# Queries and keys brought feature-first by the host; their low parts taken from SBUF by GpSimd

## The chip, the cores and the metric

One core of a Trainium2 chip. The metric is the device time of one execution in microseconds. The engines are TensorE (PE in the rows; PEld is its weight load), VectorE (DVE), ScalarE (ACT), GpSimd (POOL) and SyncE (SP), which issues all loads and stores.

## What is computed

Attention over 2 batches, 8 heads, 768 positions and 64 features per head, with a window of 96 earlier keys and 8 global ones, and then two products with a nonlinear middle for 1536 tokens of 512 features:

```python
scores = scale * q @ k^T + bias            # bias: -slope[h] * distance
scores = where(local or global, scores, -1e9)
a = exp(scores - max); a = a / (sum(a) + 1e-9)
x = a @ v                                  # heads side by side: [1536, 512]
h = x @ w_in;  x = (h * cos(h)) @ w_out    # 512 -> 2048 -> 512
out = ((x @ w_a) * (x @ w_b)) @ w_out2     # 512 -> 1536 -> 512
```

The weights are 64-bit floats in DRAM, and the kernel turns them into 32-bit ones in blocks. All products are made in parts: a value is split into a high part that TensorE takes and a low part, the rest, and the products of high with high, high with low and low with high are summed.

## The kernel before

The attention runs over 12 tiles of 128 positions, 6 for a batch. Each tile goes through steps that have short names, and a table gives each step a time, counted in tiles from the tile's own. The steps of all tiles are written in the order of these times, and TensorE, GpSimd, VectorE and ScalarE keep the written order. SyncE is not held to it: its loads are placed by the scheduler, where a buffer comes free. An engine's instruction that waits holds up all behind it.

For tile i, `LQ`, `LK`, `LV` load q, k and v as [128 positions, 8 heads, 64] (tiles nq and nk with two buffers, nv with one). `SQ` (`scale_q`) multiplies q by a factor for each head on GpSimd. `TQ` and `TK` (`turned`) transpose four pairs of heads of q and of k into PSUM on TensorE. `QH`, `KH` (`q_hi`, `k_hi`) copy that to the high parts on ScalarE. `QL`, `KL` (`q_lo`, `k_lo`) subtract the high part from the transposed value, which gives the low part. GpSimd does not read PSUM here, so QL on GpSimd needs a second copy:

```python
if QP[0] <= i < QP[1]:
    nc.scalar.activation(out=qc_of[i], in_=tq, func=AF.Copy)
```

QP is (3, 13): tiles 3 to 11 have this copy (qc) on ScalarE and QL on GpSimd; QL of tiles 0 to 2 and KL of all tiles read PSUM on VectorE. The keys of two neighbouring tiles lie in the two halves of kx. `FK` keeps the first keys of a batch in kg, and `PK`, once the scores of a tile are done, puts them in place of that tile's own first keys; both are on GpSimd. `S0` and `S1` are the scores of the two halves of the heads on TensorE; S0 of tile i + 1 needs QL and KL of i + 1 and PK of i. `B`, `E`, `T`, `H`, `L`, `P` are, for four pairs of heads each, the bias (VectorE), the exponential (ScalarE), the transpose of the weights (TensorE, tile tp), its two parts (ScalarE, VectorE) and the product with V (TensorE). `V` (`split_v`) makes three parts of V on GpSimd (tile vx; vg holds a batch's first ones, and `VG` is a DMA of them). `RL`, `FIN`, `TX`, `XH`, `XL` end the tile: VectorE, VectorE, TensorE, ScalarE, VectorE. Tile 0 is done in halves, with times of its own (`START`), and `first_bias` with the counts n_global and n_local (`read_counts`) stands between the halves on VectorE.

Between these steps the first weight blocks are loaded (raws, raw) and converted: two copies on ScalarE, four operations on VectorE (cv), and a subtraction on GpSimd (wl). Behind the attention the two products (`moe`) run, with the rest of the blocks converted as they are needed. A second, general attention exists for larger windows and is not entered with these inputs.

Of the kernel before, what the change touches and what calls it, by code (L numbers as in the profile page):

```python
# [29 lines left out]
QP = (3, 13)  # L30
# [2 lines left out]
TABLE = {'S0': -0.894, 'T3': 0.134, 'TX': 1.203, 'TQ': -1.895, 'P0': 0.161, 'TK': -1.643, 'S1': -0.525, 'P1': 0.341, 'T0': -0.22, 'T1': -0.233, 'P2': 0.506, 'P3': 0.588, 'T2': -0.085, 'RL': 0.846, 'FIN': 0.963, 'L2': 0.298, 'B0': -0.757, 'B1': -0.676, 'L3': 0.443, 'XL': 1.457, 'B2': -0.371, 'B3': -0.219, 'KL': -1.201, 'L0': 0.036, 'L1': -0.108, 'H2': 0.02, 'H3': 0.339, 'XH': 1.381, 'E0': -0.666, 'E1': -0.347, 'QH': -1.59, 'KH': -1.325, 'E2': -0.243, 'H0': -0.146, 'H1': -0.218, 'E3': -0.066, 'SQ': -2.793, 'V': -0.869, 'PK': -0.368, 'QL': -1.371, 'FK': -1.121, 'VG': 1.106, 'LQ': -4.408, 'LK': -2.688, 'LV': -1.259}
# [4 lines left out]
START_OPS = "SQ TQ QH QL TK KH KL".split()  # L38
START = ((-2.99, -2.98, -2.97, -2.96, -2.95, -2.94, -2.93), (-2.92, -2.91, -2.9, -2.86, -2.89, -2.88, -2.85))
# [8 lines left out]
def tile_kernel(ctx, tc, q, k, v, n_global, n_local, w_in, w_out, w_a, w_b, w_out2, out):  # L48
    nc = tc.nc
    B, H, S, D = q.shape  # L50
# [119 lines left out]
    qc_of = {}  # L170

    def q_hi(i, tq, hps=ALL):
        if i not in q_of:
            q_of[i] = at.tile([P, 2, HP, P], F32R, tag="qT", name=f"qT{i}", bufs=2)
        nc.scalar.activation(out=q_of[i][:, 0, hps], in_=tq, func=AF.Copy)
        if QP[0] <= i < QP[1]:
            qc_of[i] = at.tile([P, HP, P], F32, tag="qc", name=f"qc{i}", bufs=1)
            nc.scalar.activation(out=qc_of[i], in_=tq, func=AF.Copy)

    def q_lo(i, tq, hps=ALL):  # L180
        qT = q_of[i]
        if i in qc_of:
            pool_sub(qT[:, 1], qc_of.pop(i), f(qT[:, 0]))
        else:
            nc.vector.tensor_tensor(out=qT[:, 1, hps], in0=tq, in1=f(qT[:, 0, hps]), op=ALU.subtract)

    def k_hi(i, tk, hps=ALL):
        nc.scalar.activation(out=kx[:, i % 2, 0, hps], in_=tk, func=AF.Copy)

# [623 lines left out]
```

## Time and profile before

| what | value |
|---|---|
| median of 3 runs | 732.5 us (732.21 to 733.02) |
| profiled execution: span from first to last instruction | 731.0 us |
| TensorE busy, share of the span | 676.8 us, 93% |
| VectorE busy | 510.7 us, 70% |
| ScalarE busy | 303.3 us, 41% |
| GpSimd busy | 289.8 us, 40% |

The profile gives no time of its own for the profiled execution beside the span. The shares are averages over stages that differ: the attention ends near 120 us, then comes a stretch to about 260 us in which weights are converted beside the first products, and after it the products alone. What an engine is worth has to be read in its stage. TensorE's products are pipelined and their ends modelled, so that its durations overlap; the distance from one start to the next says what a group costs.

### The profile page before, as it was taken

Reading aid. Unit: us, or ns where it says so; the run is one execution under the profiler, and the core shown is the slowest. Engines: PE = TensorE matmul, PEld = TensorE weight load, DVE = VectorE, ACT = ScalarE, POOL = GpSimd, SP = SyncE. Lnnn points to the kernel's source line nnn. Section 1 sums busy time; section 2 is a strip of 40 time slices with the busy share of each in tenths; the row PEclk is TensorE's granted clock in tenths of the full one; section 3 lists DMA queues with packets and bytes.
Section 4 is the critical chain, followed back from the end, with each engine's and each line's share of the span. In section 5 each row is a group of like instructions: output and inputs, shape, how many; then the busy total and the mean of one; then the engine's idle time right before and its main releaser. Section 6 shows DMA issues by size and latency. Waiting matters only on the chain.

```text
span 731.0 us, 10359 instructions
## 1 busy us (share of the span) xinstructions
PE 676.8 (93%) x3936; PEld 556.5 (76%) x3936; DVE 510.7 (70%) x901; ACT 303.3 (41%) x559; POOL 289.8 (40%) x263
## 2 busy tenths in 40 slices
PE   4899998799885999999989698999999999999996
PEld 3778887588763788788878486888888888888885
DVE  6999898999999979859979715885727322222223
ACT  4798886554445444444454413334314111111110
POOL 5789851664444434425252404435315211111110
PEclk9999999989987799999999799999999999999998
DMA  9944320223333202201303101333301000000004
GB/s 210 249 108 107 81 48 1 86 71 103 98 103 115 87 30 87 87 1 58 105 11 109 64 0 31 106 114 95 117 1 57 1 1 0 1 1 0 1 29 150
DMA packets 65084, 49.80 MB, mean 68 GB/s; under 512 B 39168, under 2 KB 59648, under 8 KB 65024
## 3 DMA queue, kind: packets, MB, share of 16 engines
q1 hardware_dynamic: 65024, 49.04, 23.4%
q8 instruction: 33, 0.54, 0.3%
q14 instruction: 27, 0.22, 0.1%
HBM read 45.09 MB, written 3.15 MB: 66 GB/s over the span
## 4 chain that ended last, share of the span: by engine, by line
PE 50%; DVE 35%; ACT 6%; issue 4%; POOL 2%; DMA 2%; SPq 0%; POOLq 0%; ACTq 0%; DVEq 0%
DVE cv L361 6%; DVE u L436 5%; PE o L502 4%; PE o L503 4%; PE o L501 4%; DVE cv L362 4%; PE b L413 4%; PE b L412 4%; PE b L411 4%; PE a L412 4%; PE a L411 4%; PE a L413 4%; DVE u L435 4%; DVE cv L358 3%; DVE cv L360 3%
## 5 line engine op out<-in xcount | busy, mean ns | idle before, releaser
L138 POOL TENSOR_TENSOR wl<-cv,wh 128x512 fp32r<-128x512 f32 x68 | 97.1, 1431 | 167.1 <-ACT wh L368 163.9
L138 POOL TENSOR_TENSOR glu<-as,ghu 128x512 fp32r<-128x512 f32 x36 | 47.5, 1320 | 158.5 <-ACT ghu L455 158.5
L491 DVE TENSOR_TENSOR as<-b,as 128x512 f32<-128x512 f32 x36 | 24.8, 689 | 117.6 <-PE b L413 116.4
L138 POOL TENSOR_TENSOR gl<-u,gh 128x512 fp32r<-128x512 f32 x48 | 69.8, 1464 | 74.4 <-ACT gh L455 62.3
L411 PE MATMUL h<-xTh,wh 128*128 128x512 f32 x192 | 79.1, 412 | 7.6 <-ACT hs L434 5.8
L473 PE MATMUL y<-gh,wh 128*128 128x512 f32 x192 | 75.4, 393 | 9.2 <-ACT gh L455 9.2
L474 PE MATMUL y<-gl,wh 128*128 128x512 f32 x192 | 76.0, 396 | 6.4 <-POOL gl L138 6.4
L412 PE MATMUL h<-xTl,wh 128*128 128x512 f32 x192 | 79.0, 411 | 0.0
L413 PE MATMUL h<-xTh,wl 128*128 128x512 f32 x192 | 78.6, 409 | 0.0
L475 PE MATMUL y<-gh,wl 128*128 128x512 f32 x192 | 75.2, 392 | 0.0
L368 ACT ACTIVATE wh<-cv 128x512 fp32r<-128x512 f32 x68 | 42.7, 628 | 69.1 <-DVE cv L362 58.2
L440 ACT ACTIVATE u<-u,quarter 128x512 f32<-128x512 f32 x48 | 34.7, 723 | 72.1 <-DVE u L436 72.1
L507 DVE TENSOR_TENSOR oacc<-o,oacc 128x512 f32<-128x512 f32 x60 | 41.2, 690 | 31.6 <-PE o L503 31.6
L411 PE MATMUL a<-yh,wh 128*128 128x512 f32 x144 | 57.2, 398 | 6.3 <-ACT as L488 4.2
L411 PE MATMUL b<-yh,wh 128*128 128x512 f32 x144 | 57.6, 400 | 3.0 <-ACT hs L434 3.0
L488 ACT ACTIVATE as<-a 128x512 f32<-128x512 f32 x36 | 21.4, 593 | 88.6 <-PE a L413 88.6
L361 DVE SCALAR_TENSOR_TENSOR cv<-raw,cv 128x512 int32<-128x512 int32 x62 | 57.4, 926 | 0.9
L412 PE MATMUL a<-yl,wh 128*128 128x512 f32 x144 | 57.1, 396 | 0.6 <-DVE yl L482 0.6
L413 PE MATMUL b<-yh,wl 128*128 128x512 f32 x144 | 57.4, 398 | 0.0
L412 PE MATMUL b<-yl,wh 128*128 128x512 f32 x144 | 57.2, 398 | 0.0
L413 PE MATMUL a<-yh,wl 128*128 128x512 f32 x144 | 57.0, 396 | 0.0
L351 ACT ACTIVATE cv<-raw 128x512 f32<-128x512 f32 x62 | 41.4, 668 | 37.2 <-POOL wl L138 18.0
(106 smaller groups left out, 1540.7 us busy)
## 6 DMA issues: line engine op xcount, KB each, us to landing
raw<-in_moe_w_out_dram SPq DMA_DIRECT2D x26, 512.0 KB, 3.3
raw<-in_moe_w_in_dram SPq DMA_DIRECT2D x12, 512.0 KB, 3.7
raw<-in_moe_w_a_dram SPq DMA_DIRECT2D x12, 512.0 KB, 3.6
raw<-in_moe_w_b_dram SPq DMA_DIRECT2D x12, 512.0 KB, 3.6
nv<-in_v_dram SPq DMA_DIRECT2D x12, 256.0 KB, 4.3
out_dram<-oacc SPq DMA_DIRECT2D x12, 256.0 KB, 2.9
nq<-in_q_dram SPq DMA_DIRECT2D x11, 256.0 KB, 3.6
nk<-in_k_dram SPq DMA_DIRECT2D x11, 256.0 KB, 4.4
```

Of the source, the lines that this page charges most:

```text
L138: nc.gpsimd.tensor_tensor(out=dst, in0=a, in1=b, op=ALU.subtract)
L351: nc.scalar.activation(out=f(c), in_=f(top), func=AF.Abs)
L361: lambda: nc.vector.scalar_tensor_tensor(out=c, in0=top, scalar=-0x40000000, in1=c, op0=ALU.bitwise_and, op1=ALU.bitwise_or),
L368: nc.scalar.activation(out=hi, in_=f(cvs[x]), func=AF.Copy)
L411: nc.tensor.matmul(dst, wh[:, kk, :], xh[:, kk, :], start=(kk == 0), stop=False)
L412: nc.tensor.matmul(dst, wh[:, kk, :], xl[:, kk, :], start=False, stop=False)
L413: nc.tensor.matmul(dst, wl[:, kk, :], xh[:, kk, :], start=False, stop=(kk == KD - 1))
L436: nc.vector.scalar_tensor_tensor(out=u, in0=u, scalar=MAGIC, in1=hs, op0=ALU.subtract, op1=ALU.subtract)
L473: nc.tensor.matmul(yps, wh[:, m, :], gh, start=(x == 0), stop=False)
L474: nc.tensor.matmul(yps, wh[:, m, :], gl, start=False, stop=False)
L475: nc.tensor.matmul(yps, wl[:, m, :], gh, start=False, stop=(x == len(items) - 1))
L507: nc.vector.tensor_tensor(out=acc[:, u, :], in0=ops, in1=acc[:, u, :], op=ALU.add)
```

## The change

The host hands q and k over as [batch, tile, 2 x 64 features of a pair of heads, 4 pairs, 128 positions]. A tile's load is then one run of 2 KB for each of 128 partitions (1 KB for the halves of tile 0) in place of eight runs of 256 bytes, and lies in SBUF as the products need it. TQ and TK are gone, and so are their PSUM tiles and the copies qc. SQ multiplies by a factor that now differs between the upper and lower 64 partitions. QH and KH read nq and nk from SBUF. QL and KL do as well: on VectorE for tile 0, on GpSimd for all others. The buffers of nq and nk are therefore free for the next load only after QL and KL, where before they were free after TQ and TK. All other times of the table are as before. The general attention takes the new layout too.

```diff
-START_OPS = "SQ TQ QH QL TK KH KL".split()
-START = ((-2.99, -2.98, -2.97, -2.96, -2.95, -2.94, -2.93), (-2.92, -2.91, -2.9, -2.86, -2.89, -2.88, -2.85))
+START_OPS = "SQ QH QL KH KL".split()
+START = ((-2.99, -2.97, -2.96, -2.94, -2.93), (-2.92, -2.9, -2.86, -2.88, -2.85))
...
-    def load(nm, i, heads=slice(0, H)):
+    def load(nm, i, hps=slice(0, HP)):
         if i < NT // P:
             b, t = divmod(i, NQ)
             if nm not in nat.setdefault(i, {}):
-                nat[i][nm] = at.tile([P, H, D], F32, tag="n" + nm, name=f"n{nm}{i}", bufs=2 if nm != "v" else 1)
-            nc.sync.dma_start(out=nat[i][nm][:, heads], in_=srcs[nm][b, heads, t * P:(t + 1) * P, :].rearrange("h p d -> p h d"))
+                shape = [P, H, D] if nm == "v" else [P, HP, P]
+                nat[i][nm] = at.tile(shape, F32, tag="n" + nm, name=f"n{nm}{i}", bufs=2 if nm != "v" else 1)
+            if nm == "v":
+                nc.sync.dma_start(out=nat[i][nm], in_=v[b, :, t * P:(t + 1) * P, :].rearrange("h p d -> p h d"))
+            else:
+                nc.sync.dma_start(out=nat[i][nm][:, hps], in_=srcs[nm][b, t, :, hps, :])
...
-    qf = const.tile([P, H], F32, tag="qf", name="qf")
+    qf = const.tile([P, HP], F32, tag="qf", name="qf")
-        nc.gpsimd.memset(qf[:, h:h + 1], qscale / slope[h])
+        nc.gpsimd.memset(qf[(h % 2) * D:(h % 2 + 1) * D, h // 2:h // 2 + 1], qscale / slope[h])
...
     def scale_q(i, hps=ALL):
-        heads = slice(2 * hps.start, 2 * hps.stop)
-        x = nat[i]["q"][:, heads]
-        by = qf[:, heads].rearrange("p (h o) -> p h o", o=1).to_broadcast([P, heads.stop - heads.start, D])
+        x = nat[i]["q"][:, hps]
+        by = qf[:, hps].rearrange("p (h o) -> p h o", o=1).to_broadcast([P, hps.stop - hps.start, P])
         nc.gpsimd.tensor_tensor(out=x, in0=x, in1=by, op=ALU.mult)
 
-    def turned(nm, i, hps=ALL):
-        t = ps.tile([P, hps.stop - hps.start, P], F32, tag="tr", name=f"t{nm}{i}_{hps.start}", bufs=TR)
-        for x, hp in enumerate(range(hps.start, hps.stop)):
-            transpose(t[:, x, :], head(nat[i], nm, hp))
-        return t
-
-    qc_of = {}
-
-    def q_hi(i, tq, hps=ALL):
+    def q_hi(i, hps=ALL):
         if i not in q_of:
             q_of[i] = at.tile([P, 2, HP, P], F32R, tag="qT", name=f"qT{i}", bufs=2)
-        nc.scalar.activation(out=q_of[i][:, 0, hps], in_=tq, func=AF.Copy)
-        if QP[0] <= i < QP[1]:
-            qc_of[i] = at.tile([P, HP, P], F32, tag="qc", name=f"qc{i}", bufs=1)
-            nc.scalar.activation(out=qc_of[i], in_=tq, func=AF.Copy)
-
-    def q_lo(i, tq, hps=ALL):
-        qT = q_of[i]
-        if i in qc_of:
-            pool_sub(qT[:, 1], qc_of.pop(i), f(qT[:, 0]))
+        nc.scalar.activation(out=q_of[i][:, 0, hps], in_=nat[i]["q"][:, hps], func=AF.Copy)
+
+    def residue(i, dst, a, b):
+        if i == 0:
+            nc.vector.tensor_tensor(out=dst, in0=a, in1=b, op=ALU.subtract)
         else:
-            nc.vector.tensor_tensor(out=qT[:, 1, hps], in0=tq, in1=f(qT[:, 0, hps]), op=ALU.subtract)
-
-    def k_hi(i, tk, hps=ALL):
-        nc.scalar.activation(out=kx[:, i % 2, 0, hps], in_=tk, func=AF.Copy)
-
-    def k_lo(i, tk, hps=ALL):
-        nc.vector.tensor_tensor(out=kx[:, i % 2, 1, hps], in0=tk, in1=f(kx[:, i % 2, 0, hps]), op=ALU.subtract)
+            pool_sub(dst, a, b)
+
+    def q_lo(i, hps=ALL):
+        residue(i, q_of[i][:, 1, hps], nat[i]["q"][:, hps], f(q_of[i][:, 0, hps]))
+
+    def k_hi(i, hps=ALL):
+        nc.scalar.activation(out=kx[:, i % 2, 0, hps], in_=nat[i]["k"][:, hps], func=AF.Copy)
+
+    def k_lo(i, hps=ALL):
+        residue(i, kx[:, i % 2, 1, hps], nat[i]["k"][:, hps], f(kx[:, i % 2, 0, hps]))
...
-        "TQ": boxed("Q", lambda i: turned("q", i)), "QH": lambda i: q_hi(i, box["Q", i]), "QL": lambda i: q_lo(i, box.pop(("Q", i))),
-        "TK": boxed("K", lambda i: turned("k", i)), "KH": lambda i: k_hi(i, box["K", i]), "KL": lambda i: k_lo(i, box.pop(("K", i))),
+        "QH": q_hi, "QL": q_lo, "KH": k_hi, "KL": k_lo,
...
-        a = _np.ascontiguousarray(inputs[name])
+        a = inputs[name]
+        if name in ("q", "k"):
+            b, h, s, d = a.shape
+            a = a.reshape(b, h // 2, 2, s // P, P, d).transpose(0, 3, 2, 5, 1, 4).reshape(b, s // P, 2 * d, h // 2, P)
+        a = _np.ascontiguousarray(a)
```

On GpSimd, around the end of tile 8 and the start of tile 9 of V (vx: parts of V, nv: V as loaded, nq: q, qT: parts of q, kx: parts of k, kg: first keys), before:

```order
L162 TENSOR_TENSOR nq10_1441<-nq10_1441,qf_93 128x512
L138 TENSOR_TENSOR qT9_1740<-qc9_1742,qT9_1740 128x512
L141 TENSOR_SCALAR kx_81<-kg_82 128x8x32
L208 MEMSET vx9_1866 128x8x2
L141 TENSOR_SCALAR vx9_1866<-nv9_1809 128x8x64
L138 TENSOR_TENSOR nv9_1809<-nv9_1809,vx9_1866 128x512
L141 TENSOR_SCALAR vx9_1866<-nv9_1809 128x8x64
L138 TENSOR_TENSOR vx9_1866<-nv9_1809,vx9_1866 128x8x64
L162 TENSOR_TENSOR nq11_1596<-nq11_1596,qf_93 128x512
```

and with the change:

```order
L165 TENSOR_TENSOR nq10_1349<-nq10_1349,qf_93 128x512
L142 TENSOR_TENSOR qT9_1626<-nq9_1152,qT9_1626 128x512
L145 TENSOR_SCALAR kx_81<-kg_82 128x8x32
L142 TENSOR_TENSOR kx_81<-nk9_1436,kx_81 128x512
L202 MEMSET vx9_1745 128x8x2
L145 TENSOR_SCALAR vx9_1745<-nv9_1693 128x8x64
L142 TENSOR_TENSOR nv9_1693<-nv9_1693,vx9_1745 128x512
L145 TENSOR_SCALAR vx9_1745<-nv9_1693 128x8x64
L142 TENSOR_TENSOR vx9_1745<-nv9_1693,vx9_1745 128x8x64
L165 TENSOR_TENSOR nq11_1492<-nq11_1492,qf_93 128x512
```

KL of tile 9, `kx<-nk`, has come between PK and V; QL reads nq in place of qc.

On SyncE, the first loads behind those of tiles 0 and 1 (raws: weight blocks of 0.5 MB; the names in brackets are what each waits for), before:

```order
L103 DMA nv0_161<-in_v_dram 128x8x64 [waits DMAHW0_49]
L341 DMA raws0_109<-in_moe_w_in_dram 128x4x256 [waits DMAHW1_49]
L103 DMA nq2_154<-in_q_dram 128x8x64 [waits DMAHW2_49,PE_49,Pool_49]
L103 DMA nk2_197<-in_k_dram 128x8x64 [waits DMAHW5_49,DMAHW3_49,PE_49]
L341 DMA raws0_109<-in_moe_w_in_dram 128x4x256 [waits DMAHW4_49]
L103 DMA nq3_159<-in_q_dram 128x8x64 [waits PE_49,Pool_49]
L341 DMA raws1_110<-in_moe_w_in_dram 128x4x256 [waits DMAHW6_49]
```

and with the change:

```order
L105 DMA nv0_149<-in_v_dram 128x8x64 [waits DMAHW0_49]
L335 DMA raws0_109<-in_moe_w_in_dram 128x4x256 [waits DMAHW1_49]
L335 DMA raws0_109<-in_moe_w_in_dram 128x4x256 [waits DMAHW2_49]
L335 DMA raws1_110<-in_moe_w_in_dram 128x4x256 [waits DMAHW3_49]
L335 DMA raws1_110<-in_moe_w_in_dram 128x4x256 [waits DMAHW4_49]
L337 DMA raws2_111<-in_moe_w_out_dram 128x1024 [waits DMAHW5_49]
L107 DMA nq2_142<-in_q_dram 128x512 [waits DMAHW6_49,DVE_49]
L107 DMA nk2_180<-in_k_dram 128x512 [waits DMAHW7_49,DVE_49]
L337 DMA raws2_111<-in_moe_w_out_dram 128x1024 [waits DMAHW0_49]
L105 DMA nv1_217<-in_v_dram 128x8x64 [waits DMAHW1_49,Pool_49]
L107 DMA nq3_147<-in_q_dram 128x512 [waits DMAHW2_49,Pool_49]
```

The load nq2 has gone from the second place behind the first v to the sixth, behind five weight blocks, and waits for VectorE instead of TensorE.

On VectorE, ScalarE and TensorE the order shows the removed rows and no other change in the attention, and none on any engine in the products behind it, up to the general attention.

## Rows read from the trace of the kernel before

**Rows 1.** Windows view: stretch, its length, busy us (instructions) by engine, granted clock, DMA share, GB/s

```profile
0.00:10.00 10.00, 3.97 (x22) 3.11 (x23) 4.78 (x16) 2.82 (x5) 3.86 (x20) 1.00 0.74 149
10.00:20.00 10.00, 6.84 (x38) 5.23 (x38) 8.87 (x30) 5.64 (x15) 7.67 (x9) 1.00 1.17 286
...
60.00:80.00 20.00, 19.95 (x314) 17.11 (x312) 18.53 (x70) 18.17 (x45) 17.80 (x23) 1.00 0.47 107
...
140.00:260.00 120.00, 101.96 (x396) 80.83 (x397) 117.59 (x158) 55.87 (x94) 54.19 (x38) 0.89 0.31 97
260.00:731.00 471.00, 452.00 (x1960) 371.41 (x1958) 265.85 (x371) 144.03 (x241) 142.12 (x104) 0.98 0.15 48
```

**Rows 2.** Waits of GpSimd, 0 to 115 us: us in total, times, longest

```profile
POOL vx L141 <- DMA nv<-in_v_dram: 9.8, 7, 2.2
...
POOL qT L138 <- ACT qc L178: 3.1, 4, 1.1
...
POOL wl L138 <- ACT wh L368: 1.3, 1, 1.3
POOL kg L141 <- DVE rl L288: 0.7, 1, 0.7
```

**Rows 3.** Timeline of VectorE: start, us, line, operation; KL of tile 11

```profile
100.64 0.69 DVE L191 TENSOR_TENSOR kx<-tk,kx 128x512 fp32r<-128x512 f32 x1
```

**Rows 4.** Timeline of TensorE: TQ(11), S0(10), S0(11), and products behind the attention

```profile
94.06 0.60 PE L79 MATMUL tq<-ident,nq 128*128 128x128 f32 x4
94.59 0.98 PE L231 MATMUL sc<-kx,qT 64*128 64x256 f32 x12
...
101.83 0.98 PE L231 MATMUL sc<-kx,qT 64*128 64x256 f32 x12
...
121.62 0.47 PE L411 MATMUL h<-xTh,wh 128*128 128x512 f32 x1 [1.86 <-DVE xTl L320]
...
124.27 0.63 PE L413 MATMUL h<-xTh,wl 128*128 128x512 f32 x1
```

**Rows 5.** Groups by shape, 0 to 240 us: count, busy us, mean ns, idle before

```profile
L138 POOL TENSOR_TENSOR qT<-qc,qT 128x512 fp32r<-128x512 f32 x9 | 12.0, 1337 | 3.3 <-ACT qc L178 3.1
...
L79 PE MATMUL tq<-ident,nq 128*128 128x128 f32 x48 | 9.1, 316 | 10.1 <-POOL nq L162 9.2 <-DVE rl L288 0.9
...
L191 DVE TENSOR_TENSOR kx<-tk,kx 128x512 fp32r<-128x512 f32 x11 | 7.5, 685 | 0.3 <-ACT kx L188 0.2
```

**Rows 6.** Timeline of GpSimd: SQ, V(0), SQ(2); SQ(11), QL(10), PK(9); V(10), PK(10), V(11)

```profile
3.24 0.61 POOL L162 TENSOR_TENSOR nq<-nq,qf 128x256 f32<-128x256 f32 x1 [1.17 <-DMA nq<-in_q_dram]
...
11.04 0.11 POOL L208 MEMSET vx<- 128x16 bf16 x1
...
16.56 1.46 POOL L162 TENSOR_TENSOR nq<-nq,qf 128x512 f32<-128x512 f32 x1
...
90.20 1.05 POOL L162 TENSOR_TENSOR nq<-nq,qf 128x512 f32<-128x512 f32 x1
91.34 1.28 POOL L138 TENSOR_TENSOR qT<-qc,qT 128x512 fp32r<-128x512 f32 x1
92.58 0.41 POOL L141 TENSOR_SCALAR kx<-kg 128x256 fp32r<-128x256 f32 x1
...
97.27 1.13 POOL L138 TENSOR_TENSOR vx<-nv,vx 128x512 bf16<-128x512 f32 x1
...
100.45 0.42 POOL L141 TENSOR_SCALAR kx<-kg 128x256 fp32r<-128x256 f32 x1
...
102.33 0.62 POOL L141 TENSOR_SCALAR vx<-nv 128x512 bf16<-128x512 f32 x1 [1.41 <-DMA nv<-in_v_dram]
```

**Rows 7.** Timeline of SyncE: load of q for tile 2, load of V(11)

```profile
7.97 0.46 SPq L103 DMA_DIRECT2D nq<-in_q_dram  x1
...
98.43 0.37 SPq L103 DMA_DIRECT2D nv<-in_v_dram  x1
```

**Rows 8.** Windows view of TensorE alone, one microsecond behind the attention

```profile
123.00:124.00 1.00, 1.00 (x4) 0.50 0.00 0
```

More of the change, by code (lines that the diff above doesn't have):

```diff
@@ L29 @@
 SC, TR = 2, 4
[L30 removed]
 PTB = 3
[L33 removed]
+TABLE = {'S0': -0.894, 'T3': 0.134, 'TX': 1.203, 'P0': 0.161, 'S1': -0.525, 'P1': 0.341, 'T0': -0.22, 'T1': -0.233, 'P2': 0.506, 'P3': 0.588, 'T2': -0.085, 'RL': 0.846, 'FIN': 0.963, 'L2': 0.298, 'B0': -0.757, 'B1': -0.676, 'L3': 0.443, 'XL': 1.457, 'B2': -0.371, 'B3': -0.219, 'KL': -1.201, 'L0': 0.036, 'L1': -0.108, 'H2': 0.02, 'H3': 0.339, 'XH': 1.381, 'E0': -0.666, 'E1': -0.347, 'QH': -1.59, 'KH': -1.325, 'E2': -0.243, 'H0': -0.146, 'H1': -0.218, 'E3': -0.066, 'SQ': -2.793, 'V': -0.869, 'PK': -0.368, 'QL': -1.371, 'FK': -1.121, 'VG': 1.106, 'LQ': -4.408, 'LK': -2.688, 'LV': -1.259}
 BIAS = (-2.925, 0.022)
@@ L49, in tile_kernel @@
     nc = tc.nc
-    B, H, S, D = q.shape
+    B, S, D = q.shape[0], q.shape[1] * P, q.shape[2] // 2
+    H = 2 * q.shape[3]
     NT, DM = out.shape
@@ L101, in load @@
             if nm not in nat.setdefault(i, {}):
-                nat[i][nm] = at.tile([P, H, D], F32, tag="n" + nm, name=f"n{nm}{i}", bufs=2 if nm != "v" else 1)
-            nc.sync.dma_start(out=nat[i][nm][:, heads], in_=srcs[nm][b, heads, t * P:(t + 1) * P, :].rearrange("h p d -> p h d"))
+                shape = [P, H, D] if nm == "v" else [P, HP, P]
[4 more added lines that the diff above has]
+                nc.sync.dma_start(out=nat[i][nm][:, hps], in_=srcs[nm][b, t, :, hps, :])
     for half in range(2):
         for nm in "qk":
-            load(nm, 0, slice(half * H // 2, (half + 1) * H // 2))
+            load(nm, 0, slice(half * HP // 2, (half + 1) * HP // 2))
         if half == 0:
@@ L581, in general_attention @@
             for t in range(NQ):
-                kn = ga.tile([P, H, D], F32, tag="n", name=f"gk{b}_{t}")
-                nc.sync.dma_start(out=kn, in_=k[b, :, t * P:(t + 1) * P, :].rearrange("h p d -> p h d"))
+                nc.sync.dma_start(out=kT[:, :, t * P:(t + 1) * P], in_=k[b, t])
                 nc.sync.dma_start(out=vn[:, t], in_=v[b, :, t * P:(t + 1) * P, :].rearrange("h p d -> p h d"))
-                tk = gps.tile([P, HP, P], F32, tag="tr", name=f"gtk{b}_{t}", bufs=2)
-                for hp in range(HP):
-                    nc.tensor.transpose(tk[:, hp, :], kn[:, 2 * hp:2 * hp + 2, :].rearrange("p h d -> p (h d)"), ident)
-                nc.vector.tensor_copy(out=kT[:, :, t * P:(t + 1) * P], in_=tk)
             for t in range(NQ):
@@ L607, in general_attention @@
                 nc.vector.tensor_scalar(out=glb, in0=loc, scalar1=1.0e9, scalar2=-1.0e9, op0=ALU.mult, op1=ALU.add)
-                qn = ga.tile([P, H, D], F32, tag="n", name=f"gq{b}_{t}")
-                nc.sync.dma_start(out=qn, in_=q[b, :, t * P:(t + 1) * P, :].rearrange("h p d -> p h d"))
-                tq = gps.tile([P, HP, P], F32, tag="tr", name=f"gtq{b}_{t}", bufs=2)
-                for hp in range(HP):
-                    nc.tensor.transpose(tq[:, hp, :], qn[:, 2 * hp:2 * hp + 2, :].rearrange("p h d -> p (h d)"), ident)
-                qT = ga.tile([P, HP, P], F32, tag="qT", name=f"gqT{b}_{t}", bufs=1)
-                nc.vector.tensor_scalar(out=qT, in0=tq, scalar1=-qscale, scalar2=None, op0=ALU.mult)
+                qT = ga.tile([P, HP, P], F32, tag="qT", name=f"gqT{b}_{t}")
+                nc.sync.dma_start(out=qT, in_=q[b, t])
+                nc.vector.tensor_scalar(out=qT, in0=qT, scalar1=-qscale, scalar2=None, op0=ALU.mult)
                 l = ga.tile([P, H], F32, tag="l", name=f"gl{b}_{t}")
@@ L746, in tile_kernel @@
         "SQ": lambda h: scale_q(0, parts[h]),
-        "TQ": boxed("Q0", lambda h: turned("q", 0, parts[h])), "TK": boxed("K0", lambda h: turned("k", 0, parts[h])),
-        "QH": lambda h: q_hi(0, box["Q0", h], parts[h]), "QL": lambda h: q_lo(0, box["Q0", h], parts[h]),
-        "KH": lambda h: k_hi(0, box["K0", h], parts[h]), "KL": lambda h: k_lo(0, box["K0", h], parts[h])}
+        "QH": lambda h: q_hi(0, parts[h]), "QL": lambda h: q_lo(0, parts[h]),
+        "KH": lambda h: k_hi(0, parts[h]), "KL": lambda h: k_lo(0, parts[h])}
     events = [(OVER.get((x, i), i + TABLE[x]), x, fn, i) for x, fn in step.items() for i in range(NTILE) if i or x not in first]
```

## The prediction

> **What bounds the kernel now.** I read the windows view first, because each stage has a limit of its own. In 140 to 260 us VectorE is busy 117.59 of 120 us and from 260 us TensorE 452.00 of 471 [rows 1]: these stages do one fixed list of work, so a later end of the attention moves everything behind it by as much. Up to about 100 us four engines run close together: in 60 to 80 us TensorE shows 19.95, VectorE 18.53, ScalarE 18.17 and GpSimd 17.80 of 20 [rows 1]. GpSimd is the one whose idle time matters here, since it is given work. The table of its waits has 9.8 us for V loads, 3.1 for the copy qc, 1.3 for wh and 0.7 behind VectorE's rl [rows 2]. The timelines of GpSimd, VectorE and TensorE at the last tile then tell how early its keys are ready: KL(11) ends at 100.64 + 0.69 = 101.33 [rows 3] and S0(11), which needs it, starts at 101.83 [rows 4]. That is 0.5 us of slack.
>
> **What goes.** 96 transposes. Four of them hold TensorE from 94.06 until the next product at 94.59 [rows 4], so a tile loses 2 x 0.53 = 1.1 us there; the 9.1 us busy of TQ's group [rows 5] are modelled and overlap. ScalarE loses the nine copies qc. VectorE loses KL of tiles 1 to 11 and QL of tiles 1 and 2: 13 subtractions of 685 ns, 8.9 us [rows 5]. Tile 0 keeps both halves of QL and KL on VectorE. These three engines are relieved, but each gains only what the engine that they wait for lets them have.
>
> **What comes to GpSimd.** The same 13 subtractions, 128x512 with an fp32r result. The nearest row is QL's: 1337 ns mean [rows 5]; in quiet stretches the next instruction starts 92.58 - 91.34 = 1.24 us later [rows 6]. So 13 x 1.24 to 1.34 = 16.1 to 17.4 us. QL of tiles 3 to 11 stays there and now reads nq instead of qc.
>
> Does that fit into its idle time? From V(0) at 11.04 [rows 6] to the end of PK(10) at 100.45 + 0.42 = 100.87 [rows 6] are 89.8 us. The waits in between are 9.8 - 1.4 (the wait before 102.33 comes later) + 3.1 + 1.3 + 0.7 = 13.5 us [rows 2, 6]. Work: 76.3 us. With the new instructions it is 92.4 to 93.7 us, more than the 89.8 there are, even if no wait were left. KL(11) is the last of them, and S0(11) waits for it. In a plain tile GpSimd now has V, SQ, QL, PK and KL. V(10)'s last instruction ends at 97.27 + 1.13 = 98.40, its load's buffer is free then, the next V load is issued at 98.43 [rows 7] and V(11) starts at 102.33 [rows 6]: 3.9 us. SQ (1.05), QL (1.24), PK (0.41) and KL (1.24) fill those 3.9 us exactly [rows 6]. So the waits for V are not lost, they are filled, and the loop has no room left. I take no new wait there; against it stands one of 0.2 us in each of ten tiles, 2 us.
>
> Behind a late KL(i+1) stand on GpSimd V(i+1) and SQ(i+3); V(i+1) is needed a tile later and does not decide. On TensorE S0(i+1) and all behind it wait.
>
> **The start.** Without TQ and its read from PSUM the first low parts on VectorE can begin sooner, but the counts that come next wait for their own load, so little of it reaches V(0), which follows FK(0) and so KL(0). Bounds: 0, and 1.3 us (two transposes of 0.53 and a hand-over); I take 0.6, about the middle. V(0) starts at 10.4.
>
> On SyncE the loads change places: nq2 waited for a transpose and was issued at 7.97 [rows 7], behind one load of weights; now its buffer is free only when VectorE's QL(0) is done, and it stands behind five of them, 0.52 MB each. Ahead of it and with it are then 1.05 (q, k of tiles 0 and 1) + 0.26 (v) + 5 x 0.52 + 0.26 = 4.2 MB. The first 0.13 MB had landed at 3.24 [rows 6]; the rest at the 286 GB/s of 10 to 20 us [rows 1] takes 14.2 us: nq2 lands at 17.4. Before, SQ(2) ran at 16.56 [rows 6]; 0.6 earlier is 16.0, so it now waits 1.4 us, and QL(1) and KL(1) behind it. Bounds: no wait, and 3.4 us (before moved 1.49 MB in the first 10 us [rows 1], by which 4.2 MB are there at 19.4). The product S0(1), which before followed TQ(2), now follows SQ(2), QL(1) and KL(1).
>
> The Trainium skill, DMA: Bandwidth & Descriptors, Specifications, has 512 B as the least transfer for line rate and a read-modify-write below it, which speaks for the new layout (runs of 1 and 2 KB in place of 256 B). The trace agrees only in part: 256-B rows flow at 107 GB/s for a share of 0.47, that is 228 GB/s at full share, long rows at 97 for 0.31, that is 313 [rows 1], a factor of 1.4. By the rule, taken as half rate, the 1.05 MB of q and k would take 2.3 us less, nq2 would hardly wait and the time would be 733.6; by the rows it is the forecast.
>
> **The sum.** KL(11) ends at 10.4 + 93.0 + 1.4 = 104.8 instead of 101.33: 3.5 us later. The 0.5 us of slack goes first: S0(11) is 3.0 us later. Behind it VectorE, ScalarE and TensorE arrive with less left over from tile 10 than before; for that I take off 0.5 (nothing to 1.4, two VectorE operations of 0.69 [rows 3]). So +2.5 us. Against the profiled execution, whose only time is its span, 731.0, this is 733.5; the median of the runs is 732.5, 1.5 more, and so 735.0. The ends together: 92.4 of work, the earliest start, no wait for nq2 and the shorter tail give -1.1, and one more if GpSimd's other work finds VectorE less in its way (SQ's 1.46 against 1.05 [rows 6], two or three times over), -2.1; 93.7, no earlier start, 3.4 for nq2 and 2 for V loads give +8.3. That is 730.4 to 740.8.
>
> **Rivals.** *GpSimd keeps up, and the relief counts (faster).* It decides if a good part of GpSimd's 76.3 us is blocked time that goes away with VectorE's share of the work. For it: SQ took 1.46 us at 16.56, where VectorE works on weights, against 1.05 at 90.20 [rows 6]. Against: the quiet values alone already fill the loop. Point: GpSimd's work with the 13 must come under some 89 us, so 4 us less than counted. Then VectorE is the limit in 20 to 60 us and loses five KL and one QL, 6 x 0.69 = 4.1 us; later tiles gain perhaps the same again, held by ScalarE: 2 to 6 us, the time 728.5.
>
> *Nothing to measure.* nq2 comes in time, the start gains 1.3 and the tail 1.4: between -1 and +1.5 us, 732.5. For it: 0.5 us of slack and 13.5 us of waits lie close to the 16 added. A measurement of this kernel can tell about 0.2% from no change, 1.5 us.
>
> *The clock falls as well (slower still).* TensorE will wait for KL in each tile, since its own work shrinks by 1.1 us and the loop does not. After 1.86 us without work before 121.62 its products take 0.63 us [rows 4], and the granted clock is 0.50, the lower level of 1.2 GHz, where it was 1.00 [rows 8]. Against: the windows before 100 us show 1.00, gaps and all [rows 1]. The Trainium skill, TensorE: Matmul & The Clock Gate, HAM oscillation, has just this, waits in a loop that drop the clock in every pass; the trace shows it for one gap. If it held in all tiles, a tile's products would take up to twice the time and TensorE would set the loop: a microsecond more in six or so tiles, 741.
>
> That the change does not do what it says hardly can be: the written orders have no TQ, TK or qc left, and behind the attention they are unchanged.
>
> **How the numbers follow.** Forecast, GpSimd binds, +1.5 to +7 us: 0.55, likeliest 735.0, its own range 734 to 740. Nothing to measure: 0.25. Faster: 0.17. The clock: 0.03. The range leaves out most of the faster case and the clock: 730.4 to 740. Faster by over 0.2% 0.17, within it 0.25, slower 0.58.
>
> **What would show it.** Right: in 20 to 100 us GpSimd busy over 95%, its waits for V under 3 us and none for qc; TensorE's idle time ended by GpSimd's kx in most tiles; SQ(2) waiting for nq's load near 17 us; S0(11) at 104 to 105 us; VectorE at 90% or less before 100 us; unchanged lengths of the stages behind. Wrong: S0(11) before 101 us, GpSimd with idle time left and waits for V as before, or a granted clock under 1 before 100 us.

## The result and the profile after

The changed kernel takes 739.85 us (median of 5 runs, 736.9 to 741.81), the kernel before 733.02 (5 runs, 732.21 to 734.5): a ratio of 1.0085, 95% interval 1.006 to 1.011. It is slower. Its profiled execution took 738.22 us with a span of 736.4, 5.4 more than before.

Windows view of the changed kernel, columns as in [rows 1]; the stretches of [rows 1] and the rest up to 100 us:

```profile
0.00:10.00 10.00, 1.81 (x12) 1.43 (x12) 4.72 (x16) 2.73 (x5) 4.40 (x20) 1.00 0.68 193
10.00:20.00 10.00, 4.23 (x20) 3.04 (x20) 8.45 (x26) 5.59 (x15) 7.74 (x9) 1.00 0.98 332
20.00:40.00 20.00, 15.56 (x213) 13.17 (x214) 18.95 (x55) 14.13 (x33) 19.41 (x24) 1.00 0.49 147
40.00:60.00 20.00, 15.90 (x236) 14.12 (x236) 16.30 (x51) 13.78 (x29) 16.59 (x19) 0.83 0.29 86
60.00:80.00 20.00, 16.02 (x256) 14.24 (x256) 14.72 (x52) 14.73 (x35) 18.76 (x21) 0.91 0.37 100
80.00:100.00 20.00, 17.86 (x288) 15.15 (x288) 17.18 (x64) 16.88 (x39) 18.37 (x23) 1.00 0.38 106
...
140.00:260.00 120.00, 99.97 (x390) 78.49 (x389) 118.35 (x154) 57.51 (x97) 59.67 (x41) 0.89 0.30 93
260.00:736.40 476.40, 457.70 (x1989) 376.00 (x1988) 272.96 (x383) 146.38 (x245) 141.59 (x104) 0.98 0.15 49
```

GpSimd (the last busy column) is at 19.41 of 20 us in 20 to 40 us, but at 16.59 in 40 to 60, where no engine is near its limit: something else holds all of them there. The granted clock, 1.00 in every window before 100 us of the kernel before, is 0.83 and 0.91 in two.

Waits of GpSimd, 0 to 115 us, against [rows 2]:

```profile
POOL nq L165 <- DMA nq<-in_q_dram: 4.5, 4, 2.7
POOL qT L142 <- ACT qT L170: 4.0, 5, 1.8
```

The 9.8 us for loads of V are gone. In place of the 3.1 for qc stand 4.0 for QH. That copy stands on ScalarE where it stood before, ahead of qc's old place; now it comes late itself.

Timeline of GpSimd with V(0), SQ(2), and KL(11), against [rows 3, 6]:

```profile
11.18 0.12 POOL L202 MEMSET vx<- 128x16 bf16 x1
...
17.74 1.29 POOL L165 TENSOR_TENSOR nq<-nq,qf 128x512 f32<-128x512 f32 x1 [1.08 <-DMA nq<-in_q_dram]
...
108.23 1.27 POOL L142 TENSOR_TENSOR kx<-nk,kx 128x512 fp32r<-128x512 f32 x1
```

Timeline of TensorE: a product with V, S0(11), the first product of the second part, and the one behind the pause, against [rows 4]:

```profile
42.41 0.89 PE L274 MATMUL o<-vx,pt 128*128 128x65 bf16 x15 [1.68 <-DMA vx<-vg]
...
109.36 1.04 PE L225 MATMUL sc<-kx,qT 64*128 64x256 f32 x12
...
121.09 0.48 PE L405 MATMUL h<-xTh,wh 128*128 128x512 f32 x1
...
129.20 0.47 PE L405 MATMUL h<-xTh,wh 128*128 128x512 f32 x1 [1.93 <-DVE xTl L314]
```

The first product of the second part in the kernel before:

```profile
113.59 0.48 PE L411 MATMUL h<-xTh,wh 128*128 128x512 f32 x1
```

S0(11) is 7.5 us later than before (109.36 for 101.83), and so is the second part (121.09 for 113.59). The waits of TensorE name what had not been there to this degree: in 20 to 125 us it waited 9.3 us, five times, for the transfer of the first values (VG, a copy of a batch's first values into the tile vx by DMA); before it was 1.2 us, once. After, and before:

```profile
PE o L274 <- DMA vx<-vg: 9.3, 5, 2.2
```

```profile
PE o L280 <- DMA vx<-vg: 1.2, 1, 1.2
```

Why is that transfer late? SyncE issues it, in its own order. Timeline of SyncE in the changed kernel: the load of k for tile 5, then VG:

```profile
39.11 0.33 SPq L107 DMA_DIRECT2D nk<-in_k_dram  x1
39.53 0.62 SPq L294 DMA_DIRECT2D vx<-vg  x1
```

and on GpSimd KL(3), which reads the buffer that this load fills:

```profile
37.82 1.26 POOL L142 TENSOR_TENSOR kx<-nk,kx 128x512 fp32r<-128x512 f32 x1
```

KL(3) ends at 39.08, the load goes at 39.11, VG behind it at 39.53, and TensorE's product goes on at 42.41. In the kernel before the same load was issued at 33.22, since TensorE's transpose TK(3), not a subtraction, made the buffer free, and VG 2 us behind it:

```profile
33.22 0.37 SPq L103 DMA_DIRECT2D nk<-in_k_dram  x1
...
35.46 0.62 SPq L300 DMA_DIRECT2D vx<-vg  x1
```

The table of SyncE's waits shows the same for loads of q. Before, in 0 to 125 us, seven waits for TQ on TensorE:

```profile
SPq L103 <- PE tq L79: 15.3, 7, 3.1
```

after, eight waits for QL on GpSimd:

```profile
SPq L107 <- POOL qT L142: 24.2, 8, 4.9
```

TensorE's late products with V hold ScalarE in turn: its step H writes into a tile (pt) that they make free. In 0 to 125 us it waited there 9.0 us, before 1.6:

```profile
ACT pt L257 <- PE o L274: 9.0, 6, 2.6
```

QH stands behind such steps on ScalarE, and GpSimd waits for QH. So the chain is closed: GpSimd is behind, holds the loads, they hold VG, VG holds TensorE, TensorE holds ScalarE, and ScalarE holds GpSimd. What follows on TensorE is in the windows of two microseconds around the wait before 42.41 (TensorE alone is of interest: first busy column and clock):

```profile
40.00:42.00 2.00, 0.74 (x9) 0.63 (x10) 2.00 (x9) 1.36 (x3) 1.83 (x3) 1.00 0.49 182
42.00:44.00 2.00, 1.59 (x19) 1.39 (x18) 1.37 (x3) 0.60 (x1) 2.00 (x2) 0.64 0.02 4
44.00:46.00 2.00, 2.00 (x19) 1.64 (x19) 1.98 (x4) 1.76 (x4) 0.84 (x2) 0.51 0.56 127
```

After the wait the granted clock falls to the lower level, 1.2 GHz, and TensorE, now busy all the time, does 19 products in 2 us.

### The profile page after: what moved, and what is told of

The parts are those of the page before. It is cut to its first block, busy times and chain, and to the rows that moved or that the text cites. A ratio compares the mean times of both kernels' runs of the same rounds, so it can differ in the third digit from the quotient of the medians.

```text
span 736.4 us, 10160 instructions
## 1 busy us (share of the span) xinstructions
PE 666.2 (90%) x3840; PEld 547.7 (74%) x3840; DVE 506.0 (69%) x888; ACT 300.9 (41%) x550; POOL 306.4 (42%) x276
## 3 DMA queue, kind: packets, MB, share of 16 engines
HBM read 45.09 MB, written 3.15 MB: 66 GB/s over the span
## 4 chain that ended last, share of the span: by engine, by line
PE 46%; DVE 31%; POOL 9%; ACT 5%; issue 4%; DMA 3%; SPq 0%; POOLq 0%; ACTq 0%; DVEq 0%
DVE cv L355 6%; DVE u L430 5%; PE o L497 4%; PE o L495 4%; PE o L496 4%; DVE u L429 4%; PE b L405 4%; PE b L406 4%; PE a L406 4%; PE b L407 4%; PE a L405 4%; PE a L407 4%; DVE cv L356 4%; DVE cv L352 3%; DVE cv L354 3%
```

## Experiments

Two causes were to be told apart: the time that the moved subtractions take on GpSimd, and the place of VG on SyncE. Each expectation says what its letters stand for; they change from one to the next. Times of products are from the one profiled execution of each run, ratios from all executions.

**VG ahead of the loads of k.**

```diff
+                if nm == "k" and last_vg:
+                    tc.add_manual_dep(x.ins, last_vg[0], mybir.DependencyInfo(mybir.DependencyClass.NoSync, mybir.DependencyReason.DATA),
+                                  reason="first values first")
...
-            nc.sync.dma_start(out=vx_of[i][:GLOB], in_=vg_of[i // NQ])
+            last_vg[:] = [nc.sync.dma_start(out=vx_of[i][:GLOB], in_=vg_of[i // NQ]).ins.name]
```

> The change with one thing added: on SyncE the load of a tile's k stands behind the DMA of a batch's first values (VG) that comes before it in the table, and no longer ahead of it. GpSimd's work is the same. Theory A (GpSimd's 13 added subtractions alone cost the time): the wait of TensorE for vx<-vg goes, but GpSimd still sets the pace; at most 1 us less than the change, 738.5 to 740. Theory B (part of the loss is VG, held on SyncE behind loads of k that wait for KL on GpSimd): TensorE's 9.3 us of waits for vx<-vg fall below 4, ScalarE's QH comes sooner, GpSimd's waits for QH fall from 4.0 to under 1.5, and 2 to 4 us come back, 736 to 738.

Measured: 736.58 us (4 runs, 736.02 to 737.86), ratio 1.0068 (1.0051 to 1.0085). TensorE's wait for VG and the windows of 40 to 80 us:

```profile
PE o L278 <- DMA vx<-vg: 1.2, 3, 0.6
```

```profile
40.00:60.00 20.00, 17.32 (x280) 14.09 (x277) 19.71 (x57) 16.15 (x36) 18.11 (x21) 1.00 0.38 103
60.00:80.00 20.00, 15.96 (x278) 13.87 (x277) 15.47 (x62) 15.73 (x39) 19.23 (x22) 1.00 0.33 88
```

The wait is nearly gone, the clock stays at 1.00 there, and GpSimd is now full (18.11 and 19.23 of 20). The first product of the second part comes at 117.94 instead of 121.09:

```profile
117.94 0.48 PE L409 MATMUL h<-xTh,wh 128*128 128x512 f32 x1
```

So VG's place is a part of the loss, some 3 of 7.5 us in the profile, and behind it stands GpSimd. In the time alone this part is not clear of noise: the intervals of the two ratios, 1.0068 and 1.0085, overlap.

**KL on VectorE.** All of KL, and QL of tiles 0 to 2, on VectorE, reading SBUF.

```diff
-        residue(i, kx[:, i % 2, 1, hps], nat[i]["k"][:, hps], f(kx[:, i % 2, 0, hps]))
+        residue(i, kx[:, i % 2, 1, hps], nat[i]["k"][:, hps], f(kx[:, i % 2, 0, hps]), 99)
```

> The change with the split of the engines as it was before: KL of all tiles and QL of tiles 1 and 2 on VectorE, now from SBUF, QL of tiles 3 to 11 on GpSimd. The transposes and the copies stay away. Theory A (GpSimd is the limit): S0(11) at 98 to 101 us and 727 to 731, below the kernel before, since TensorE and ScalarE are relieved; VectorE is at 97% or more again in 20 to 60 us. Rival (the transposes and copies were hidden anyway, VectorE sets the pace): 731 to 734. Theory B alone would leave GpSimd's share without effect and give what e1 gives.

Measured: 734.76 us (6 runs, 732.87 to 738.17), ratio 1.0037 (1.001 to 1.0064). Better than the change, but not better than before, and outside the range of Theory A and of its rival; S0(11) starts at 103.21. VectorE is full now:

```profile
20.00:40.00 20.00, 15.81 (x191) 12.86 (x193) 19.63 (x57) 13.55 (x32) 16.57 (x20) 1.00 0.45 141
40.00:60.00 20.00, 16.94 (x265) 13.60 (x263) 19.93 (x58) 15.62 (x34) 15.77 (x19) 1.00 0.36 101
```

It was as full before:

```profile
20.00:40.00 20.00, 18.09 (x254) 15.28 (x252) 19.73 (x61) 15.86 (x37) 15.10 (x21) 1.00 0.85 223
40.00:60.00 20.00, 18.65 (x299) 15.99 (x300) 19.93 (x61) 16.84 (x37) 17.52 (x20) 1.00 0.43 97
```

KL from SBUF takes it 1043 ns on average where KL from PSUM took 685 [rows 5]: 11 x 0.36 = 3.9 us more on an engine without any to give. That this makes the loss is argued, not shown: the profiled execution is one of the fastest of the six (733.08), with a span of 730.5 us.

**Three buffers for q**, so that its loads wait less for QL.

```diff
-                nat[i][nm] = at.tile(shape, F32, tag="n" + nm, name=f"n{nm}{i}", bufs=2 if nm != "v" else 1)
+                nat[i][nm] = at.tile(shape, F32, tag="n" + nm, name=f"n{nm}{i}", bufs={"q": 3, "k": 2, "v": 1}[nm])
```

> The change with three buffers for q in place of two: the load of q for tile 2 is free to be issued at once, ahead of the weight blocks, and SQ(2) no longer waits (1.1 us in the change); later loads of q do not wait for QL. If the late start counts in full, S0(1) comes 1 to 2 us sooner than 21.7 and the time is 737.5 to 739. If GpSimd has the first tiles' work anyway and VG is still behind k, nothing: 739 to 740.5.

Measured: 740.93 us (4 runs, 739.64 to 741.64), ratio 1.0118 (1.0101 to 1.0135). No gain, though S0(1) goes on at 20.58 us, 1.15 us sooner than in the change. TensorE still waits 8.2 us for VG, which here too comes behind loads of k.

**Transposes put back, with nothing that reads them.** TQ and TK are made on TensorE from the new nq and nk, and their result is not used.

```diff
+        "TQ": lambda i: turned("q", i), "TK": lambda i: turned("k", i),
```

> The change with the transposes of q and k of tiles 1 to 11 put back on TensorE at their old places, into PSUM tiles that nothing reads. Theory A and B: TensorE had time to spare, 0 to 1.5 us more than the change, 739.5 to 741.5. Clock theory (TensorE falls to the lower level for lack of work, 0.83 in 40 to 60 and 0.91 in 60 to 80 us, and that costs time and spreads the runs): granted clock 1.00 up to 100 us, 2 to 4 us less than the change, and runs closer together.

Measured: 739.4 us (4 runs, 738.17 to 740.37), ratio 1.0098 (1.008 to 1.0116), the same as without them. The work that TensorE is rid of is not the cause. The clock did not hold at 1.00 as that theory wanted, either: it is 1.00 in 40 to 60 us, but 0.91 in 60 to 80, and the waits for VG are still there. What the lower clock costs by itself no run here tells.

**Only q laid out by the host.**

```diff
+                shape = [P, HP, P] if nm == "q" else [P, H, D]
...
+        sub = nc.gpsimd if QP[0] <= i < QP[1] else nc.vector
```

> Only q is laid out on the host; k is transposed, evicted and subtracted out of PSUM as before, and VectorE keeps the low parts of q for tiles 0 to 2, GpSimd those of tiles 3 to 11. Theory A (the loss is the low part of k, moved to GpSimd and read from SBUF): GpSimd has as many subtractions as before, TensorE loses 48 transposes and ScalarE nine copies that nobody waited for, so 729 to 733 us, GpSimd no busier than before between 20 and 100 us. Theory B (the loss is the start, where the second tile's q is issued behind four weight blocks): that stays, so 735 to 738 us, the first scores of tile 1 near 21 us. Theory C (TensorE with fewer transposes is granted a lower clock): about half the loss, 735 to 737 us, with a granted clock under 1.00 between 40 and 100 us.

Measured: 735.51 us (5 runs, 735.01 to 736.55), ratio 1.004 (1.0027 to 1.0054). GpSimd does no more than before (63.94 us busy in 20 to 100 us, before 64.98), and still half of the loss is there, so Theory A is not the whole. Nor is the start: the products of S0(1) run at 15.94 us in one go, and up to S0(9) at 86.39 the scores are at most 1.6 us behind those of the kernel before. The clock is 0.91 in 80 to 100 us, as Theory C has it. But in that window VG comes late, behind a load of q, and behind that wait the scores are 3.2 us late (S1(9) at 93.82 for 90.58):

```profile
90.26 0.98 PE L276 MATMUL o<-vx,pt 128*128 128x65 bf16 x15 [1.83 <-DMA vx<-vg]
```

**Only k laid out by the host.**

```diff
+                shape = [P, HP, P] if nm == "k" else [P, H, D]
...
+        sub = nc.gpsimd if i else nc.vector
```

> Only k is laid out on the host, with its low part on GpSimd from tile 1 on; q is transposed, evicted and subtracted as before. Theory A: GpSimd gets the eleven subtractions of k (14 us) on top of all it had, so nearly all of the loss is here: 737 to 741 us, GpSimd over 95% busy from 20 to 100 us and the last KL near 108 us. Theory B: the load of the third tile's q stands ahead of the weight blocks again, so 732 to 735 us. Theory C: 735 to 737 us.

Measured: 738.63 us (4 runs, 736.98 to 740.19), ratio 1.0089 (1.0072 to 1.0105): the whole loss, with the last KL at 106.67 us. The time is the one of Theory A; but GpSimd was busy for 72.24 of 80 us, 90% and not 95, and TensorE waited 5.5 us for VG.

**KL left out of tiles 2 to 11.**

```diff
     def k_lo(i, hps=ALL):
+        if i > 1:
+            return
```

> The changed kernel, but the low part of k is worked out for tiles 0 and 1 only; the ten others use what stands in the buffer. GpSimd does 12.7 us less. Theory A: the loss goes, and what TensorE and ScalarE were relieved of shows, if it is worth anything: 726 to 731 us, no wait of TensorE for the first values. Theory B: 735 to 738 us. Theory C: 735 us or more, with the granted clock as low as in the changed kernel between 40 and 80 us.

Measured: 735.2 us (8 runs, 733.68 to 738.66), ratio 1.0037 (1.0018 to 1.0056). That is not Theory A; the time lies where Theories B and C meet, and the clock is as C has it. With ten subtractions fewer GpSimd is busy for 11.91 of 20 us in 40 to 60 us, and the kernel is still slower than before:

```profile
40.00:60.00 20.00, 15.59 (x232) 13.47 (x231) 15.45 (x50) 13.52 (x29) 11.91 (x16) 0.83 0.29 83
```

```profile
PE o L276 <- DMA vx<-vg: 6.3, 4, 3.2
```

```profile
119.12 0.48 PE L407 MATMUL h<-xTh,wh 128*128 128x512 f32 x1
```

So "GpSimd has no time" is not the whole of it. The load of q still waits for QL, VG still stands behind the loads of q and k, and the clock falls as in the changed kernel. (Leaving KL out takes work from GpSimd and, at once, a wait from S0; the two were not told apart.) C had fallen with the idle transposes, which did not bring the time back. This led to a theory of two causes that cover for each other, Theory D below.

**Both together**: KL left out of tiles 2 to 11, and VG ahead of the loads of q and k.

```diff
+        if i > 1:
+            return
...
+        if nm in "qk" and last_vg:
+            tc.add_manual_dep(x.ins, last_vg[0], mybir.DependencyInfo(mybir.DependencyClass.NoSync, mybir.DependencyReason.DATA),
+                          reason="first values first")
```

> Both at once: the low part of k is left out for tiles 2 to 11 (GpSimd does 12.7 us less than in the changed kernel) and SyncE issues each load of q or k behind the transfer of the first values that comes before it in the program. Theory D (two causes side by side: GpSimd has no time for the subtractions of k, and the transfer of the first values stands on SyncE behind loads whose buffers GpSimd now frees, so that TensorE waits for it): each alone took away a part only, because the other took over; both together give 728 to 731.5 us, TensorE waits under 2 us for the first values, and the second part starts its first product at 112 to 114 us. Theory E (the loss that is left is the start, where the first scores of tile 1 come at 21.7 us instead of 19.1 us): 733.5 to 736 us, the first product of the second part at 116 us or later.

Measured: 731.05 us (12 runs, 729.67 to 734.91), ratio 0.9987 (0.9972 to 1.0002). The loss is gone. Waits of TensorE from 20 us on (for VG a little over the 2 us that Theory D allowed), and the first product of the second part:

```profile
PE sc L234 <- POOL kx L149: 5.1, 1, 5.1
PE o L283 <- DMA vx<-vg: 2.1, 2, 1.1
```

```profile
113.02 0.48 PE L414 MATMUL h<-xTh,wh 128*128 128x512 f32 x1
```

The late start is still there: S0(1) goes on at 21.50 us after a wait of 5.1 (5.4 in the changed kernel), where before it starts at 19.13. At the end nothing of it is left. Whether the loop had slack for it, or the work that TensorE, ScalarE and VectorE are rid of paid for it, was not told apart. Theory E falls, and D stands; C falls once more, since there are no transposes here and the clock is 1.00 in all windows from 20 to 120 us.

What the edge does in the trace is less than its name: it moves loads of k only. A load of q, five tiles ahead, comes before VG in the program, and SyncE still issues VG right behind it, here as in the other runs with VG ahead that have q's new layout:

```profile
47.56 0.33 SPq L113 DMA_DIRECT2D nq<-in_q_dram  x1
47.98 0.52 SPq L303 DMA_DIRECT2D vx<-vg  x1
48.60 0.53 SPq L113 DMA_DIRECT2D nk<-in_k_dram  x1
```

This VG landed 2.9 us after its issue. Without the edge (KL left out alone) the same one was issued at 47.70, behind both loads, and landed after 4.6 us; but one of the changed kernel, issued at 48.59 behind a load of q alone, took 4.6 us as well. So the load of k is a part of VG's delay, and what the load of q still ahead of it costs was not tried. In one table, with the start of the second part's first product in brackets (113.59 before):

| | VG behind the loads of q and k | VG ahead of the load of k |
|---|---|---|
| KL on GpSimd | 1.0085 (121.09) | 1.0068 (117.94) |
| KL of tiles 2 to 11 left out | 1.0037 (119.12) | 0.9987 (113.02) |

Down either column, and along the lower row, the intervals of the ratios do not overlap; along the upper row they do.

**VG ahead, in the kernel before.** The same edge on the loads, nothing else.

> The kernel before, with nothing changed but SyncE's order: each load of q or k behind the transfer of the first values that comes before it in the program. Theory D: before, the buffers of q and k were freed by TensorE's transposes, in time, so the transfer waited for no engine that was behind and its place is worth at most the one wait of 1.2 us: 731 to 733 us. If the place of the transfer is worth something by itself, whatever frees the buffers: 727 to 730 us.

Measured: 731.46 us (12 runs, 729.48 to 732.82), ratio 0.9987 (0.9974 to 0.9999); TensorE waits nowhere for VG. At best 1 us, as Theory D has it: where transposes free the buffers, VG's place hardly matters. It is also the fastest kernel of this study that does all the work, by as much as can just be measured. And it has the same ratio as the previous run, which had no transposes, no qc and almost no KL. So what the change takes from TensorE, ScalarE and VectorE, less what its late start costs, comes to nothing that these runs can tell.

**Attempts at a version that is faster with the new layout.** First only q by the host, with VG ahead:

> Only q laid out on the host, and the transfers of the first values ahead of the loads of q and k that follow them in the program. Theory D: GpSimd has no more subtractions than before and the transfer comes in time, so 729 to 732.5 us, no stall between 80 and 100 us, VectorE as busy there as before. Theory E: the start is as in the run with q alone, so the time too, 734.5 to 736.5 us.

Measured: 733.45 us (12 runs, 732.73 to 736.39), ratio 1.0023 (1.0008 to 1.0037). The median is two microseconds below the run without the edge, but the intervals of the ratios overlap, and it is one microsecond short of what Theory D gave. TensorE waited for VG as long as without the edge (2.5 us): VG still stands right behind loads of q, so this run was no test of a VG in time. In the profiled execution, one of the four slower ones (735.65), the loss arises at the longer of these waits: S0(9) is 0.4 us behind the kernel before, S1(9) 1.9. For the median this stays open.

Then KL on VectorE for even tiles and on GpSimd for odd ones, with VG ahead:

> The changed layout for q and k, the low part of k on VectorE for the even tiles and on GpSimd for the odd ones, that of q on VectorE for tiles 0 to 2, and the transfers of the first values ahead of the loads. Theory D: 7.5 us of subtractions on GpSimd and 5 us on VectorE fit beside what they have, so 730 to 733 us and the first product of the second part at 113 to 115 us. Theory E: 734 to 737 us.

Measured: 736.46 us (11 runs, 732.82 to 737.76), ratio 1.0039 (1.0024 to 1.0054). The runs lie 5 us apart, and the profiled one is near their fast end (733.21), so its trace, with 3.8 us of waits for VG, does not explain the median, which lies in Theory E's range. This stays open too.

Last the same with V's first step, a copy, moved from GpSimd to ScalarE:

```diff
-        pool_copy(vx[:, :, 0:D], vn)
+        nc.scalar.activation(out=vx[:, :, 0:D], in_=vn, func=AF.Copy)
```

> The changed layout for q and k with the load spread: the low part of k on VectorE for even tiles and on GpSimd for odd ones, that of q on VectorE for tiles 0 to 2, the transfers of the first values ahead of the loads, and the first of the four steps on V (a copy, 0.62 us) on ScalarE, which no longer makes the nine copies of q. GpSimd then has about as much as before, VectorE a little less, ScalarE some 2 us more. Theory D: 729 to 733 us, no slower than before and at best 3 us faster. If an engine that is in order cannot take a step that waits for a load without holding what stands behind it: 734 to 738 us, with ScalarE waiting for V.

Measured: 741.39 us (4 runs, 740.91 to 741.95), ratio 1.013 (1.0108 to 1.0152), worse than either expectation. The wait is on the other side of the hand-over. Waits of GpSimd, 0 to 125 us:

```profile
POOL nv L149 <- ACT vx L210: 9.8, 4, 3.9
POOL nv L149 <- issue: 9.1, 4, 4.1
```

GpSimd, relieved of 12 x 0.62 = 7.4 us, now waits at V's second step: 9.8 us that the profile puts down to ScalarE's copy, and 9.1 us in front of the same instruction for which it names no cause. ScalarE itself waited for a load of V only once, 1.6 us.

## Why the prediction was right and wrong

The direction was right, and the time, 739.85, lies just inside the upper end of the range (730.4 to 740). That is partly luck. The size was not right: +5.4 us of span for +2.5, and S0(11) at 109.36 us, where the forecast had 104 to 105. The range reached that far by a longer wait for nq2 (up to 3.4 us; it was 1.08) and 2 us of waits for V that did not come; what filled it was another wait.

- **What comes to GpSimd: right in kind.** KL takes 1273 ns on average and QL 1366, forecast 1240 to 1340, and the waits for V are filled. With VG ahead of the loads of k GpSimd is full up to 100 us, and the second part starts 117.94 - 113.59 = 4.35 us late, where the sum had 2.5 to 3.0. Without KL and with most of VG's wait gone nothing is lost. That term was the right mechanism, somewhat small.
- **"I take no new wait there": this is the step that failed.** SyncE's order was followed for nq2, at the start, and not through the tiles. That the buffers of nq and nk are free only after QL and KL stood among the facts of the change, with no price. In a kernel where GpSimd runs late, every load into such a buffer runs late, and VG, which has nothing to do with q and k, is issued behind them. TensorE waited 9.3 us for it. Putting VG ahead of the loads of k alone gave 121.09 - 117.94 = 3.15 us in the profiles, and where KL is out 119.12 - 113.02 = 6.1 us.
- **"GpSimd busy over 95%": wrong.** 73.13 of the 80 us from 20 to 100, 91%. It waited for QH, which came late because TensorE did. With VG ahead of the loads of k it is 95%. TensorE's idle time was not ended by kx in most tiles either: VG ended most of it from 40 us on.
- **The start: right for nq2, wrong for V(0).** nq2 had landed at 17.74, forecast 17.4, and SQ(2) waited 1.08 us, forecast 1.4. V(0) began at 11.18, not at 10.4, so the 0.6 us to be gained were not there. S0(1) came 2.6 us late (21.73 for 19.13). The run with both causes removed has about the same late start and the time of before, so that the start's term need not show at the end; whether it was paid for by less work elsewhere is open.
- **The clock: wrong as priced.** The rival had 0.03, with "the windows before 100 us show 1.00, gaps and all" against it, and a granted clock under 1 before 100 us was named as a sign of being wrong. The changed kernel has 0.83 and 0.91 in two windows. There it fell behind waits for VG, so that it follows from the step that failed; with VG ahead of the loads of k those two windows show 1.00 while GpSimd is full. But it is not VG alone that brings it. In that same run it fell in 80 to 100 us (0.91), behind 0.85 us in front of scores that waited for GpSimd (the profile names the memset that follows KL there), while a wait of 2.25 us for the same at 75.67 us left it at 1.00:

```profile
83.29 0.85 PE L229 MATMUL sc<-kx,qT 64*128 64x256 f32 x10 [0.85 <-POOL vx L206]
```

```profile
84.00:86.00 2.00, 2.00 (x29) 1.87 (x26) 1.82 (x8) 0.91 (x2) 1.83 (x3) 0.57 0.55 135
```

In the kernel before with VG ahead, which has all its transposes, it fell too, to 0.50 in 30 to 32 us, behind a wait of 1.90 us for ScalarE:

```profile
27.65 0.84 PE L79 MATMUL tp<-ident,sp 128*128 128x128 f32 x4 [1.90 <-ACT sp L256]
```

The Trainium skill, TensorE: Matmul & The Clock Gate, HAM oscillation, has waits that drop the clock in every pass of a loop; here it fell behind some of the waits and not behind all: at 63.75 us TensorE had waited 1.69 us for VG, and the clock stayed at 1.00 from 62 to 66.

- **Later stages of unchanged length: off by 2 us.** From its first product to the end of the span the second part took 736.4 - 121.09 = 615.3 us, before 731.0 - 113.59 = 617.4. Before, its clock was 0.50 around 123 us [rows 8]; the changed kernel has 1.00 from 120 to 140 us. That does not explain the difference: in the run with idle transposes the clock falls there again (0.91 in 120 to 140 us), and the stage takes 737.9 - 121.32 = 616.6 us, but the run with q alone has 1.00 there and takes 734.1 - 117.06 = 617.0. The cause stays open.
- **"GpSimd keeps up, and the relief counts": not borne out.** With hardly any KL to do and VG ahead of the loads of k the kernel takes what the kernel before takes with VG ahead (ratio 0.9987 both times). The 2 to 6 us did not appear, not even there. That start is 2.4 us later than before (S0(1) at 21.50 for 19.13), and relief may have made that up; which engine sets the loop then was not tried.

## What to carry to other kernels

When a change alters which engine last reads a load's buffer, follow that buffer's queue through the whole loop: every transfer that is issued behind the load inherits the new engine's delay, also those that carry something else. Where two causes cover for each other, removing each alone shows a part or nothing; only the run with both removed tells whether anything of the loss is left. And look in the trace whether an edit of the order did what it was named for: here it moved the loads of k and not those of q.

## What the runs showed of the hardware

A subtraction with both operands in SBUF is not one price on VectorE. In the run with KL on VectorE it took 1.53 us beside a subtraction on GpSimd and 0.69 us while GpSimd waited. VectorE:

```profile
56.36 1.53 DVE L174 TENSOR_TENSOR kx<-nk,kx 128x512 fp32r<-128x512 f32 x1
...
65.11 0.69 DVE L174 TENSOR_TENSOR kx<-nk,kx 128x512 fp32r<-128x512 f32 x1
```

and GpSimd at the same times:

```profile
56.23 1.12 POOL L142 TENSOR_TENSOR nv<-nv,vx 128x512 f32<-128x512 f32 x1
...
65.89 0.41 POOL L145 TENSOR_SCALAR kg<-kx 128x256 fp32r<-128x256 f32 x1 [1.02 <-DVE rl L282]
```

GpSimd's subtraction ends at 57.35, and 0.54 us later VectorE's ends, at 57.89. The Trainium skill, SBUF — State Buffer, Who interferes with whom, says that a VectorE instruction with two inputs in SBUF and a GpSimd instruction that reads SBUF exclude each other for a whole instruction. This trace agrees. With the transposed value in PSUM there was no such price (685 ns on average [rows 5]).

The runs of one kernel differ with the clock that they are granted: the five of the changed kernel have spans of 735.0 us at a mean of 0.974, 736.4 at 0.965, 738.1 at 0.958, and 739.7 and 739.9 at 0.956.
